# A 20-product scheme for the first expert layer, with three accumulators moved to DRAM and more accumulation on ScalarE

## The chip, the cores and the metric

The kernel runs on one core of one Trainium2 chip. The metric is device time in microseconds for one launch. A profiled execution gives a trace of every instruction; TensorE is called PE in it, its weight loads PEld, VectorE DVE, ScalarE ACT, GpSimd POOL, and SP is the engine that issues most DMAs.

## The reference

Linear attention with the feature map elu + 1 is followed by a mixture of eight experts. The weights of the experts for a token come from a Sinkhorn iteration over all tokens, so they are known only when the attention of all tokens is done.

```python
# attention: 8 batches, 8 heads, 576 tokens, 64 per head
q_p, k_p = phi(q), phi(k)                       # phi(x) = elu(x) + 1
kv = einsum('bhsd,bhse->bhde', k_p, v);  z = sum(k_p, axis=2)
x = einsum('bhsd,bhde->bhse', q_p, kv) / (einsum('bhsd,bhd->bhs', q_p, z)[..., None] + 1e-06)
# x becomes 4608 tokens x 512
P = exp(x @ w_gate - max)                       # 4608 x 8
for _ in range(8):
    P /= P.sum(1, keepdims=True) + 1e-09
    P /= P.sum(0, keepdims=True) + 1e-09
    P *= N / E
for e in range(8):
    h = maximum(x @ w1[e], 0)                   # 512 -> 1024
    out += P[:, e:e + 1] * (h @ w2[e])          # 1024 -> 512
```

## The kernel before

**Order of work.** Everything is emitted by a planner, the class `_Plan`. A task has an engine (or a choice of two), a cost in us, dependencies, buffers that it takes from pools, and a priority; `run` goes through the tasks in planned time and emits the instructions of each engine in that order. [...] A table `ranks` overrides the priority or the engine of single tasks by their number. For TensorE the order of the expert part is written out by hand: the list `order` names the products of one unit and its neighbours, and a chain of dependencies makes the planner keep it.

**Stages.** The front computes the attention for one batch and four heads at a time and writes x, transposed and in fp16, to `xT`. Expert 0 runs while the front is still going on, with plain matmuls (`layer1`, L546, and `unit_plain`, L736), because its result can be scaled by P afterwards (L757). The Sinkhorn iteration runs on VectorE meanwhile. Then come experts 1 to 7, each in nine units of 512 tokens.

**A unit of experts 1 to 7.** Both layers use a scheme of 7 products in place of 8 for a 2x2 by 2x2 block product (the Strassen-Winograd form).

- First layer (`block7`): sums of x are made once, on VectorE (`x_blocks`, L579), and stored in DRAM in `xd`. For each unit SP loads 896 KB of them back (L598). Sums of w1 (`combos`, W, L783) are made once per expert. In two halves of the hidden columns, seven products of four 256-column matmuls each run in PSUM (L640). ScalarE copies partial results (L652, L656, L660) and does two of the four relus (L663, L666); VectorE does the other two as "add, then relu" from PSUM and SBUF (L669).
- Second layer (`unit`): VectorE makes four sums S of the hidden values (L816), 128x1024 each; T holds the sums of w2 (L795). Seven products of eight matmuls (L843) run in three banks, X, R and Z. Product 1 is copied once to seed Z (L878). Six results are then scaled by P and added to `acc`: five by VectorE in one operation from PSUM (L857), one by ScalarE, which scales into a buffer `st` (L864), and POOL, which adds it (L867).

The accumulators `acc` of all nine units lie in SBUF. The very last unit of expert 7 uses plain matmuls for its second layer (L736 and L720), so that its rows can be written out one after the other.

**Buffers.** PSUM has eight banks: two of the pool "hq", two of "att", ye0 and ye1 (X and R), ye2 (Z) and ye3 (the first layer's third bank). Weights are double-buffered and loaded by POOL (L207), cast from fp32 to fp16 on the way.

The only lines of the hand-written order:

```python
order = "y1 y5 y2 a7 y6 y3 a4 b1 b5 y7 b6 b3 b2 b7 A1 A5 y4 b4 A6 A3 A2".split()
final = "y1 y5 y2 y6 a7 y3 a4 b1 b5 y7 b6 b3 b2 b7 y4 b4".split()
```

Here y are second-layer products of the unit before, a and b the first-layer products of the two halves, and capitals belong to the next unit.

Of the kernel before, what the change touches and what calls it, by code (L numbers as in the profile page):

```python
# [16 lines left out]

class _Plan:
# [10 lines left out]

    def grp(self, pool):  # L30
        return {"pool": pool, "users": [], "tile": None}

# [19 lines left out]
    def run(self):  # L52
# [11 lines left out]
        def slot(t):  # L64
            r = t["ready"]
            seen = {}
            for g in t["acq"]:
                o, n = g["pool"]["order"], g["pool"]["n"]
                i = len(o) + seen.get(id(o), 0)
                seen[id(o)] = i + 1 - len(o)  # L70
                if i >= n:
                    for u in o[i - n]["users"]:
                        d = self.t[u]["done"]
                        if d is None:
                            return None
                        r = max(r, d + self.LAT.get(self.t[u]["on"], 0.06))
            return r

        while left:
# [28 lines left out]
            for g in t["acq"]:  # L108
                g["pool"]["order"].append(g)
# [13 lines left out]
def kernel(  # L123
# [10 lines left out]
    nc = tc.nc  # L134
# [21 lines left out]
    hpool = ctx.enter_context(tc.tile_pool(name="hpool", bufs=2))  # L156
# [5 lines left out]
    xpool = ExitStack()  # L162
    xp = xpool.enter_context(tc.tile_pool(name="xp", bufs=1, side="right"))

    xT = xp.tile([P, NDT, N], FP16, tag="xT", name="xT")
    NXB = 7 * 512
    xd = [dpool.tile([P, NXB], FP16, tag=f"xd{g}", name=f"xd{g}") for g in range(NG)]
# [6 lines left out]
    ones_t = const.tile([P, P], FP32, tag="ones", name="ones_t")  # L174

# [9 lines left out]
    p_att, p_hq, p_h = S_.pool(2), S_.pool(2), S_.pool(2)  # L185
    p_T, p_S, p_W, p_xs, p_xst, p_s2, p_s5 = (S_.pool(2) for _ in range(7))
    p_st = S_.pool(3)
    p_z = S_.pool(1)
    p_w1, p_w2 = S_.pool(2), S_.pool(2)
    p_ye = [S_.pool(1) for _ in range(4)]  # L190

    def load_w(ten, nm, pl, ap, cut, e, prio, parts=1, after=0.0, deps=()):
# [6 lines left out]
        for i in range(parts):  # L199
# [8 lines left out]
            ti = add(("pool", 1.0), fn, use=[g], prio=prio, deps=[tal])  # L208
            ts_.append(add(("dma", 6.0 / parts), lambda _: None, deps=[ti], use=[g], prio=prio, lat=2.6))
            w_last[0] = ti  # L210
        return g, [ts_[0], ts_[-1]]

    def load_w1(e, **kw):
        return load_w(moe_w1, "w1", p_w1, [[F, P], [F * P, NDT], [1, F]], 2, e, **kw)
# [22 lines left out]
    def att(b, g):  # L237
# [146 lines left out]
        for c2 in range(2):  # L384
# [8 lines left out]
            def f_xc(e, c2=c2, gx=gx):  # L393
                copy(e, xT[:, 2 * g + c2, S * b:S * b + S], gx["tile"])
# [6 lines left out]
    def logits(b2):  # L401
        gl = S_.grp(p_att)

        def f_l(_):
            gl["tile"] = aps.tile([P, NJ, E], FP32, tag="att", name="lg_ps")
            for i in range(NJ):
                for c in range(NDT):
                    nc.tensor.matmul(gl["tile"][:, i, :], lhsT=xT[:, c, ts(NJ * b2 + i, P)], rhs=wg_sb[:, c, :],
                                     start=(c == 0), stop=(c == NDT - 1))
# [8 lines left out]
    def sinkhorn():  # L418
# [9 lines left out]
        for it in range(8):  # L428
# [13 lines left out]
            gc = S_.grp(p_att)  # L442

            def f_c(_, gc=gc):
                gc["tile"] = aps.tile([P, E], FP32, tag="att", name="cs_ps")
# [61 lines left out]
    Zt = [None, None]  # L507

    def f_close(_):
# [4 lines left out]
        accp.append(ctx.enter_context(tc.tile_pool(name="combo", bufs=2)))  # L514
        for i, n in enumerate(("ye2", "ye3")):
            Zt[i] = yps.tile([P, 2, 256], FP32, tag=n, name=f"Z{n}")
            nc.tensor.matmul(Zt[i].rearrange("p a b -> p (a b)"), lhsT=warm[:, 0:P], rhs=warm, start=True, stop=True)
# [3 lines left out]
    hcount = [0]  # L521
    fin_prev = {}
    w_next = {}

    def layer1(e, g):
        gw1, tw1, gw2, tw2 = w_t[e]
        bs = range(512 * g // S, (512 * g + 511) // S + 1)
        xd_ = [xt_done[(b, c)] for b in bs for c in range(NDT)]
        th = []
        gh = S_.grp(p_h)  # L530

        def f_ha(_):
            gh["tile"] = hpool.tile([P, NFT, 512], FP16, tag="h", name="h")
        tha = add(("none", 0.0), f_ha, deps=[prev_hq[0]], acq=[gh], prio=g - 400.0)
# [4 lines left out]
        for f, c0, c1 in jobs:  # L539
            ghq = ghqs[f]  # L540

            def f_hq(_, f=f, ghq=ghq, c0=c0, c1=c1):
                if c0 == 0:
                    ghq["tile"] = hqp.tile([P, 512], FP32, tag="hq", name="hq")
                for c in range(c0, c1):
                    nc.tensor.matmul(ghq["tile"], lhsT=gw1["tile"][:, c, ts(f, P)], rhs=xT[:, c, ds(512 * g, 512)],  # L546
                                     start=(c == 0), stop=(c == NDT - 1))

            def f_rl(_, f=f, ghq=ghq):
                nc.scalar.activation(out=gh["tile"][:, f, :], in_=ghq["tile"], func=AF.Relu)  # L550
# [4 lines left out]
            x_users.append(t1)  # L555
# [3 lines left out]
        return gh, [th, th]  # L559

    def x_blocks(g):
        bs = range(512 * g // S, (512 * g + 511) // S + 1)
        deps = [xt_done[(b, c)] for b in bs for c in range(NDT)]
        t0 = 512 * g
        gt_ = S_.grp(p_xst)

        def f_raw(_):
            nc.sync.dma_start(out=xd[g][:, 0:512].rearrange("p (c t) -> p c t", c=2), in_=xT[:, 0:2, t0:t0 + 256])
            nc.sync.dma_start(out=xd[g][:, 512:1536].rearrange("p (c t) -> p c t", c=2), in_=xT[:, 2:4, t0:t0 + 512])
        last = None  # L570
        for i in range(4):
            def f_T(_, i=i):
                if i == 0:
                    gt_["tile"] = accp[1].tile([P, 4, 2, 256], FP16, tag="xst", name="xst")
                T = gt_["tile"]
                b11, b12 = xT[:, 0:2, t0:t0 + 256], xT[:, 0:2, t0 + 256:t0 + 512]
                b21, b22 = xT[:, 2:4, t0:t0 + 256], xT[:, 2:4, t0 + 256:t0 + 512]
                a0, a1 = [(b12, b11), (b22, T[:, 0]), (b22, b12), (b21, T[:, 1])][i]
                nc.vector.tensor_tensor(out=T[:, i], in0=a0, in1=a1, op=ALU.subtract)  # L579
            last = add(("dve", 0.42), f_T, deps=deps + [t_close, last], acq=[gt_] if i == 0 else [], use=[gt_],  # L580
                       prio=g - 8.0)
            x_users.append(last)

        def f_st(_):
            nc.sync.dma_start(out=xd[g][:, 1536:NXB], in_=gt_["tile"].rearrange("p i c t -> p (i c t)"))
        ti = add(("sp", 0.45), f_st, deps=[last], use=[gt_], prio=0.0)
        out_ = [add(("dma", 1.5), lambda _: None, deps=[ti], use=[gt_], prio=0.0, lat=2.6)]
        ti = add(("sp", 0.9), f_raw, deps=deps + [t_close, ti], prio=0.0)
        out_.append(add(("dma", 1.0), lambda _: None, deps=[ti], prio=0.0, lat=2.6))
        x_users.append(out_[1])  # L590
        return out_

    def x_load(e, g):
        gr = S_.grp(p_xs)

        def fn(_):
            gr["tile"] = accp[1].tile([P, NXB], FP16, tag="xs", name="xs")
            nc.sync.dma_start(out=gr["tile"], in_=xd[g])  # L598
        ti = add(("sp", 0.1), fn, acq=[gr], deps=xd_done[g] + [t_close, xs_prev[0]], prio=e * NG + g)
        xs_prev[0] = ti  # L600
        return gr, add(("dma", 3.0), lambda _: None, deps=[ti], use=[gr], prio=e * NG + g, lat=2.6)

    def block7(e, g, gW, tW):
        gw1, tw1, gw2, tw2 = w_t[e]
        ui = e * NG + g
        gxs, txs = x_load(e, g)
        gh = S_.grp(p_h)
        th = [[], []]

        def f_ha(_):  # L610
            gh["tile"] = hpool.tile([P, NFT, 512], FP16, tag="h", name="h")
        tha = add(("none", 0.0), f_ha, deps=[prev_hq[0]], acq=[gh], prio=ui - 400.0)

        def A(i, j, gi):
            return lambda p, c: gw1["tile"][:, 2 * (j - 1) + c, ts(4 * (i - 1) + 2 * gi + p, P)]

        def W(i, gi):
            return lambda p, c: gW["tile"][:, i - 1, c, ts(2 * gi + p, P)]

        def Bx(o, w):  # L620
            return lambda c: gxs["tile"][:, o + w * c:o + w * c + 256]

        def T(i):
            return Bx(1536 + 512 * (i - 1), 256)
        B11, B21, B22 = Bx(0, 256), Bx(512, 512), Bx(768, 512)

        def pair(gi):
            gX, gR, gZ, gs2, gs5 = (S_.grp(p) for p in (p_hq, p_att, p_ye[3], p_s2, p_s5))
            kx = {id(gX): (hqp, "hq"), id(gR): (aps, "att")}
            f0 = 2 * gi  # L630

            def pm(lhs, rhs, g_, first, deps, pr):
                def f_m(_):
                    if first:
                        pl, tag = kx[id(g_)]
                        g_["tile"] = pl.tile([P, 2, 256], FP32, tag=tag, name=tag)
                    dst = Zt[1] if g_ is gZ else g_["tile"]
                    for p in range(2):
                        for c in range(2):
                            nc.tensor.matmul(dst[:, p, :], lhsT=lhs(p, c), rhs=rhs(c),  # L640
                                             start=(first and p == 0 and c == 0), stop=(c == 1), skip_group_check=True)
                return add(("pe", 0.436), f_m, deps=deps, acq=[g_] if first else [], use=[g_, gw1, gW, gxs],
# [363 lines left out]
```

The softmax here doesn't subtract the row's maximum and nothing guards it: scores larger than these inputs give would overflow.

## Time and profile before

| | |
|---|---|
| Device time, two runs | 970.89 and 974.2 us, median 972.55 |
| Span of the profiled execution | 970.4 us, 21442 instructions |
| Granted TensorE clock | 0.999 |
| Busy: PE, DVE, ACT, POOL | 959.5, 776.5, 575.0, 112.2 us |
| HBM read and written | 119.69 MB and 17.69 MB |

The span runs from the first to the last instruction of the profiled execution; the device time of a run contains a little more on both sides, and is here between 0.5 and 3.8 us longer than the profiled span. A busy time counts an engine once where two of its records overlap. The mean duration of an instruction in the groups is longer than its step in a full queue, because the next one starts before it ends.

### The profile page before, as it was taken

The numbers are of one execution on the slowest core, as the hardware profiler recorded it, in microseconds if no ns is written. First come the engines' busy times: TensorE is split into PE (matmuls) and PEld (weight loads), VectorE is DVE, ScalarE is ACT, GpSimd is POOL, SyncE is SP. The second block draws the span as 40 slices with busy tenths as digits, with TensorE's granted clock in tenths as the row PEclk, the third lists the DMA queues.
The fourth block names the chain that finished last, engine by engine and source line by source line (L and its number), as shares of the span: only waits on it lengthen the run. The fifth ranks groups of instructions, "written<-read, shape, count | busy, mean of one in ns | idle before, by whom it ended". The sixth has DMA issues, their size and how long they took to land.

```text
span 970.4 us, 21442 instructions
## 1 busy us (share of the span) xinstructions
PE 959.5 (99%) x8737; PEld 794.4 (82%) x8737; DVE 776.5 (80%) x1563; ACT 575.0 (59%) x1049; POOL 112.2 (12%) x158
## 2 busy tenths in 40 slices
PE   8999999999999999999999999999999999999998
PEld 4556564588888888888888888888888888888886
DVE  6899868988887888878887888878887888877775
ACT  6799945465555555555555555555555555555553
POOL 3000000101111111111111111111111111111110
PEclk9999999999999999999999999999999999999999
DMA  9986925472226222272226222272226322235554
GB/s 312 265 271 243 243 73 207 155 162 76 78 76 138 99 74 74 79 152 78 73 75 138 98 73 78 76 161 77 78 77 137 104 77 77 77 96 166 163 163 110
DMA packets 47188, 121.99 MB, mean 126 GB/s; under 512 B 4208, under 2 KB 18288, under 8 KB 47088
## 3 DMA queue, kind: packets, MB, share of 16 engines
q1 hardware_dynamic: 32208, 99.76, 30.2%
q0 software_dynamic: 14480, 20.33, 11.8%
q8 instruction: 68, 1.11, 0.4%
q10 hardware_dynamic: 400, 0.52, 0.2%
q14 instruction: 32, 0.26, 0.1%
HBM read 119.69 MB, written 17.69 MB: 142 GB/s over the span
## 4 chain that ended last, share of the span: by engine, by line
PE 92%; DMA 3%; ACT 3%; DVE 1%; issue 1%; POOL 0%; ACTq 0%; DVEq 0%; POOLq 0%
PE ye L843 33%; PE hq L640 23%; PE att L640 11%; PE ye L736 6%; PE Zye L640 6%; PE Zye L843 6%; PE hq L546 4%; DMA w<-in_moe_w_dram 2%; PE yw L481 1%; DMA kin<-in_k_dram 1%; PE xt_ps L390 1%; ACT eq L266 1%; ACT h L550 1%; PE kv_ps L309 1%; PE num_ps L374 1%
## 5 line engine op out<-in xcount | busy, mean ns | idle before, releaser
L857 DVE SCALAR_TENSOR_TENSOR acc<-ye,P_sb,acc 128x256 f32<-128x256 f32 x620 | 267.2, 479 | 128.2 <-PE ye L843 127.7
L640 PEld LDWEIGHTS <-W 128*128 128x128 f16 x2016 | 197.2, 98 | 23.6
L843 PEld LDWEIGHTS <-S 128*128 128x128 f16 x1984 | 194.1, 98 | 22.5
L843 PE MATMUL ye<-T,S 128*128 128x256 f16 x1488 | 192.9, 273 | 0.0
L640 PEld LDWEIGHTS <-w 128*128 128x128 f16 x1512 | 147.9, 98 | 18.5 <-issue 0.8
L666 ACT ACTIVATE h<-hq 128x512 f16<-128x512 f32 x126 | 75.2, 597 | 144.1 <-PE hq L640 144.1
L843 PEld LDWEIGHTS <-h 128*128 128x128 f16 x1488 | 145.6, 98 | 16.9
L867 POOL TENSOR_TENSOR acc<-acc,st 128x256 f32<-128x256 f32 x124 | 87.5, 727 | 621.4 <-ACT st L864 562.5
L640 PE MATMUL hq<-xs,W 128*128 128x256 f16 x1008 | 151.3, 273 | 0.0
L640 PE MATMUL att<-xs,W 128*128 128x256 f16 x1008 | 151.3, 273 | 0.0
L640 PE MATMUL hq<-xs,w 128*128 128x256 f16 x1008 | 141.0, 273 | 0.4 <-DVE h L669 0.3
L663 ACT ACTIVATE h<-Zye 128x512 f16<-128x512 f32 x126 | 75.2, 597 | 40.6 <-PE Zye L640 40.6
L864 ACT ACTIVATE st<-Zye,P_sb 128x256 f32<-128x256 f32 x124 | 52.0, 470 | 78.3 <-PE Zye L843 78.3
L669 DVE CUSTOM_DVE_ANT_0 h<-att,s 128x512 f16<-128x512 f32 x126 | 86.6, 687 | 11.4 <-ACT s L656 11.0
L656 ACT COPY s<-hq 128x512 f32<-128x512 f32 x126 | 73.4, 583 | 36.7 <-PE hq L640 36.7
L816 DVE TENSOR_TENSOR S<-h 128x1024 f16<-128x1024 f16 x124 | 85.2, 687 | 12.3 <-ACT h L666 12.3
L669 DVE CUSTOM_DVE_ANT_0 h<-hq,s 128x512 f16<-128x512 f32 x126 | 86.6, 687 | 0.2
L652 ACT COPY Zye<-hq 128x512 f32<-128x512 f32 x126 | 73.2, 581 | 17.5 <-PE hq L640 17.5
L736 PE MATMUL ye<-w,h 128*128 128x512 f16 x312 | 75.6, 379 | 1.9 <-DMA w<-in_moe_w_dram 1.4
L640 PE MATMUL Zye<-xs,w 128*128 128x256 f16 x504 | 75.7, 273 | 0.0
L660 ACT COPY s<-att 128x512 f32<-128x512 f32 x126 | 74.7, 593 | 0.0
L546 PE MATMUL hq<-xT,w 128*128 128x512 f16 x288 | 70.3, 379 | 0.9 <-ACT h L550 0.7
(95 smaller groups left out, 961.2 us busy)
## 6 DMA issues: line engine op xcount, KB each, us to landing
xs<-xd SPq DMA_DIRECT2D x63, 896.0 KB, 4.6
w<-in_moe_w_dram POOLq DMA_DIRECT2D x14, 1024.0 KB, 11.4
out_dram<-acc SPq DMA_DIRECT2D x67, 128.0 KB, 2.4
kin<-in_k_dram SPq DMA_DIRECT2D x14, 576.0 KB, 5.8
qin<-in_q_dram SPq DMA_DIRECT2D x14, 576.0 KB, 5.5
vin<-in_v_dram SPq DMA_DIRECT2D x14, 576.0 KB, 5.8
xd<-xst SPq DMA_DIRECT2D x9, 512.0 KB, 2.7
xd<-xT SPq DMA_DIRECT2D x9, 256.0 KB, 3.1
```

The source lines that it names most:

```text
L546: nc.tensor.matmul(ghq["tile"], lhsT=gw1["tile"][:, c, ts(f, P)], rhs=xT[:, c, ds(512 * g, 512)], start=(c == 0), stop=(c == NDT - 1))
L640: nc.tensor.matmul(dst[:, p, :], lhsT=lhs(p, c), rhs=rhs(c), start=(first and p == 0 and c == 0), stop=(c == 1), skip_group_check=True)
L656: nc.scalar.copy(out=gs2["tile"], in_=gX["tile"])
L660: nc.scalar.copy(out=gs5["tile"], in_=gR["tile"])
L663: nc.scalar.activation(out=hd(0, 0), in_=Zt[1], func=AF.Relu)
L666: nc.scalar.activation(out=hd(1, 0), in_=gX["tile"], func=AF.Relu)
L669: nc.vector._custom_dve(TENSOR_ADD_SAT, out=dst, in0=ps, in1=sb, s0=3.0e38, s1=0.0)
L736: nc.tensor.matmul(gy[tt]["tile"], lhsT=gh["tile"][:, f, ds(P * tt, P)], rhs=gw2["tile"][:, f, :], start=(f == 0), stop=(f == NFT - 1))
L816: nc.vector.tensor_tensor(out=Sx[:, i], in0=a0, in1=a1, op=op)
L843: nc.tensor.matmul(bank(g_)[:, s, :], lhsT=lhs(s, kk), rhs=rhs(kk), start=(new and s == 0 and kk == 0), stop=(kk == 3), skip_group_check=True)
L857: nc.vector.scalar_tensor_tensor(out=dst(), in0=bank(g_)[:, s, :], scalar=P_sb[:, gg, e:e + 1], in1=dst(), op0=ALU.mult, op1=ALU.add)
L867: nc.gpsimd.tensor_tensor(out=dst(), in0=dst(), in1=gst["tile"], op=ALU.add)
```

## The change

The first layer of experts 1 to 7 is computed in units of 768 tokens, six in all, with a scheme of 20 products in place of 24 for a block product of 4x2 (w1: four blocks of hidden columns, two of inputs) by 2x3 (x: two of inputs, three of tokens). The second layer keeps its units of 512 tokens and its seven products. Two first-layer units and three second-layer units make one round of 1536 tokens; `ORDER` lists the 61 products of a round, each with the round that it belongs to relative to the others, and this list replaces `order` and `final`.

- `A_SUM` lists 15 sums of w1 blocks, `B_SUM` 13 sums of x blocks; `A_OF` and `B_OF` say which operands a product takes. The x blocks are stored to DRAM one by one in the order of their use (`xd` is now three sets of ten tiles of four blocks) and loaded four at a time (512 KB), into three and later six buffers.
- `STEPS` lists what happens with the products of a first-layer unit: 2 seeds and 8 saves by ScalarE, 2 relus by ScalarE (`ev0`), 10 add-relus (`ev1`) and 2 additions to a saved value (`savex`) by VectorE. The products run in five PSUM banks, so ye3, hq and att are shared by eight short chains.
- Of the six scaled results of a second-layer unit, four go through ScalarE and `st` and two (products 5 and 6) through VectorE. For units 0 to 4 and 8, POOL adds what is in `st` to `acc` in SBUF, 512 columns at a time, and VectorE accumulates its two directly. For units 5, 6 and 7 the accumulator lies in DRAM (`accd`), VectorE also scales into `st`, and POOL issues an accumulating DMA. The SBUF space of these three blocks holds T and two S buffers.
- Expert 0's blocks are scaled by P on ScalarE instead of VectorE. The weights of experts 2 to 7 are loaded in quarters, one per unit. The last unit is no longer plain. The small Sinkhorn matmul uses ye2 in place of "att". `xT` is split in three tiles whose space is reused for `sb` (saved values), `st` and three xs buffers. Entries of `ranks` above task 659 are gone.

The core of the diff:

```diff
+PRODUCTS = [(3, [2, 7, 15]), (4, []), (6, [5, 8]), (4, [3, 4]), (5, [4, 9]), ...
+ORDER = [(53, -2), (7, -1), (19, -1), (36, -2), (18, -1), (50, -2), (51, -2), (9, -1), (54, -2), ...
+    DG = (5, 6, 7)
+    accd = {g: dpool.tile([P, 4, 512], FP32, tag=f"ad{g}", name=f"ad{g}") for g in DG}
...
-                nc.vector.tensor_scalar(out=acc[g][:, tt, :], in0=acc[g][:, tt, :],
-                                        scalar1=P_sb[:, gg, 0:1], scalar2=None, op0=ALU.mult)
+                nc.scalar.mul(out=acc[g][:, tt, :], in_=acc[g][:, tt, :], mul=P_sb[:, gg, 0:1])
...
+    def hk1(e, v, afs):
+        for p in uo:
+            def f_m(_, p=p, c=c, n=n, sx=sx, new=new):
+                for pf in range(2):
+                    for kt in range(2):
+                        nc.tensor.matmul(bank(c)[:, pf, :], lhsT=lhs(p, pf, kt), rhs=own["xs"][sx][:, n % XC, kt, :],
+                                         start=(new and pf == 0 and kt == 0), stop=(kt == 1), skip_group_check=True)
...
+        for i, (kind, c, dst, src, dp, de, sg) in enumerate(STEPS):
+            def f_e(_, i=i, kind=kind, c=c, dst=dst, src=src, sg=sg):
+                if kind == "seed" or kind == "save":
+                    ... nc.scalar.copy(out=o, in_=bank(c)) or nc.scalar.mul(out=o, in_=bank(c), mul=-1.0)
+                elif kind == "savex":
+                    nc.vector.scalar_tensor_tensor(out=own["sb"][...], in0=bank(c), ... in1=own["sb"][...])
+                elif kind == "ev0":
+                    nc.scalar.activation(out=o, in_=bank(c), func=AF_.Relu, scale=float(sg[0]))
+                else:
+                    nc.vector._custom_dve(TENSOR_ADD_SAT, out=o, in0=bank(c), in1=own["sb"][...], s0=3.0e38, s1=0.0)
...
+        def ev(g_, ti, dh, dep, on_act):
+            if gst is None:
+                ... two nc.vector.scalar_tensor_tensor into acc, as before
+            else:
+                def f_e2(_):
+                    for s in range(2):
+                        if on_act:
+                            nc.scalar.mul(out=dst, in_=bank(g_)[:, s, :], mul=sc)
+                        else:
+                            nc.vector.tensor_scalar(out=dst, in0=bank(g_)[:, s, :], scalar1=sc, scalar2=None, op0=ALU.mult)
+                def f_g(_):
+                    st = own["st"][:, gst["slot"]]
+                    if g in DG:
+                        nc.gpsimd.dma_start(out=half(accd[g], ti, dh), in_=st, accum_op=ALU.add)
+                    else:
+                        dst = half(acc[g], ti, dh)
+                        nc.gpsimd.tensor_tensor(out=dst, in0=dst, in1=st, op=ALU.add)
```

## The prediction

> **What bounds the kernel now.** I read the page first (busy shares, the chain of waits), then the stages of 20 us, then the groups, and last the timelines of single engines.
>
> ```profile
> PE 959.5 (99%) x8737; PEld 794.4 (82%) x8737; DVE 776.5 (80%) x1563; ACT 575.0 (59%) x1049; POOL 112.2 (12%) x158
> ...
> PE 92%; DMA 3%; ACT 3%; DVE 1%; issue 1%; POOL 0%; ACTq 0%; DVEq 0%; POOLq 0%
> ...
> 500.00:520.00 20.00, 20.00 (x185) 17.91 (x184) 15.57 (x31) 11.20 (x22) 2.67 (x5) 1.00 0.12 47
> ```
>
> TensorE is 92% of the chain, and in every slice from 120 to 940 us it is busy 20.00 of 20.00 (the last line: PE, PEld, DVE, ACT, POOL, clock, DMA share, GB/s). Busy PE need not be PE at its peak, so I count: the chain shows eight 256-column matmuls in 0.87 us, 0.109 each. A unit of 512 tokens has 56 + 56 of them, 12.2 us, and POOL's first additions of two units start 12.23 us apart. So there is no stall left; only fewer matmuls make the middle shorter, and each new stall costs its full length.
>
> ```profile
> 499.77 1.41 POOL L867 TENSOR_TENSOR acc<-acc,st 128x256 f32<-128x256 f32 x2 [10.81 <-ACT st L864]
> 512.00 1.42 POOL L867 TENSOR_TENSOR acc<-acc,st 128x256 f32<-128x256 f32 x2 [10.82 <-ACT st L864]
> ...
> 508.67 0.68 DVE L669 CUSTOM_DVE_ANT_0 h<-att,s 128x512 f16<-128x512 f32 x1
> 509.27 0.68 DVE L816 TENSOR_TENSOR S<-S,h 128x1024 f16<-128x1024 f16 x1
> 509.87 0.69 DVE L816 TENSOR_TENSOR S<-h 128x1024 f16<-128x1024 f16 x1
> 510.49 0.88 DVE L857 SCALAR_TENSOR_TENSOR acc<-ye,P_sb,acc 128x256 f32<-128x256 f32 x2
> 511.28 0.68 DVE L816 TENSOR_TENSOR S<-h,S 128x1024 f16<-128x1024 f16 x1
> ...
> 511.44 0.84 ACT L864 ACTIVATE st<-Zye,P_sb 128x256 f32<-128x256 f32 x2 [1.26 <-PE Zye L843]
> ```
>
> The second fence gives prices. Starts on a busy VectorE lie 0.60 us apart (a 0.68 us record overlaps the next one), 0.40 for half of an accumulation pair; xst sums start 0.35 apart at 179 us. ScalarE's copies start 0.50 apart at 502 us; a scaled pair takes 0.84. A POOL addition of 256 columns fills 0.71.
>
> [...]
>
> ```profile
> 181.79 10.38 DVE L757 TENSOR_SCALAR acc<-acc,P_sb 128x512 f32<-128x512 f32 x26
> ...
> 188.91 3.57 POOL L207 DMA_DIRECT2D w<-in_moe_w_dram  x1 [73.20 <-PE hq L546]
> ...
> L207 POOL DMA_DIRECT2D w<-in_moe_w_dram x18: 745/838/3570, 8.7 to 746.1; - x18
> ```
>
> An issue with a median of 0.84 us took 3.57 and ended at 192.48, just after VectorE's row of 26 ended at 192.17. The form that matters here, S on VectorE against an addition on POOL, never coincides in the kernel before: each addition starts as the fourth S ends (the S at 511.28 ends 511.96, POOL starts 512.00). [...]
>
> **The change, part by part,** in rounds of 1536 tokens (3 old units, 36.7 us; 21 rounds).
> 1. *Fewer matmuls.* First layer: 63 units x 56 = 3528 become 42 x 80 = 3360. The last unit loses its plain form: 24 of 512 columns and 16 of 256 (64 equivalents) become 56. Together 176 x 0.109 = **-19.2 us**. A round is now 40 x 0.4365 + 21 x 0.873 = 35.8 us.
> 2. *VectorE.* Before: 12 add-relus, 12 S, 30 accumulations, 8/3 W and T: 12 x 0.60 + 12 x 0.60 + 30 x 0.40 + 1.6 = 28.0 of 36.7 us. After: 24 add-relus and savex, 12 S, 12 accumulating or scaling reads, 5 weight sums at 0.35, 4/3 T: 14.4 + 7.2 + 4.8 + 1.75 + 0.8 = 28.9 of 35.8 (81%). It fits: nothing on the path by load alone.
> 3. *ScalarE.* 33 copies x 0.50 + 3 pairs x 0.84 = 19.0 becomes 27 x 0.50 + 12 x 0.84 = 23.6 of 35.8 (66%). Nothing by load. From the written order I took, for each product, the PE time between the one before it in its bank and itself: the shortest gaps are three slots of 0.4365 = 1.31 us, against 0.10 + 0.85 for a pair. They just hold.
> 4. *POOL.* Per expert 24 additions of 512 columns (1.41 each, as two of 256) and 18 accumulating issues and 8 weight issues at 0.84: 56 of 107 us. An addition is no longer placed behind the fourth S. A round has 18.3 two-input VectorE operations; additions hold POOL 31% of the time; a blocked one waits half of 1.41: 18.3 x 0.31 x 0.70 = 4.0 us of VectorE delay per round. Its idle 6.9 us can take this, and S has about 3 us between the last h and the first product that needs it; but VectorE's narrow waits (y6 to y7: 1.75 us with 1.1 needed) cannot take a whole block queued in front. Bounds: nothing to 2 us per round on PE. I take 0.25, **+5 us**.
> 5. *DMA.* The queue table (packets, MB, share of 16 engines' span; q1 is SP's, q0 POOL's):
>
> ```profile
> q1 hardware_dynamic: 32208, 99.76, 30.2%
> q0 software_dynamic: 14480, 20.33, 11.8%
> ...
> xs<-xd SPq DMA_DIRECT2D x63, 896.0 KB, 4.6
> ```
>
>    That is 0.302 x 970.4 / 99.76 = 2.94 us per MB for SP and 5.63 for POOL. A round loads 5.24 MB of xs: 15.4 us, in six buffers that are each due only every 21 us, against 4.6 us for a landing today: hidden. In units 5 to 7 come 18 accumulations of 0.26 MB and three weight quarters (4.4 us): 35.8 - 15.4 - 4.4 leaves 0.89 us for each. At SP's rate one takes 0.77 and all hide; at POOL's 1.48 they don't. I take the hidden end, since POOL's queue so far carried weights that are cast from twice the bytes they land as: 0.
> 6. *Start of the rounds.* 78 x sums replace 36 and 120 stores replace 27. Scaling expert 0's blocks leaves VectorE (36 x 0.40) for ScalarE. In the first full round TensorE has only 40 + 10 products, 26.2 us, and VectorE 14.4 + 4.8 + 1.6 + 1.75 + some 20 late sums x 0.35, about 30. Bounds 0 to 6; **+3 us**. The front loses the tuned ranks of tasks above 659; PE waits little there now, bounds -1 to 4; **+1 us**.
> 7. *Last round.* y7, P16, y4, y5, y1, y3, y6, y7, y2, y4, y5, y3 stand close: a pair on ScalarE or VectorE needs about 1.1 us from product to product, and what stands between covers 0.44, 0.87, 0, 0.87 and 0: 0.6 + 0.2 + 1.1 + 0.2 + 1.1 = **+3.2 us**. The last block then goes ScalarE pair, POOL addition (0.95 + 1.41) where one VectorE operation of 0.48 stood: **+1.8 us**.
>
> Sum against the profiled span: 970.4 - 19.2 + 5 + 3 + 1 + 3.2 + 1.8 = 965.2. The median of the runs shown, 972.55, lies 2.15 above that span, so 967.4, say **967 us**.
>
> **Rivals.**
> - *All hidden:* additions fall beside harmless work, the start costs nothing: 967 - 5 - 3 - 1 = 958, and 955 if the last round overlaps better. For it: PE has no stall in the whole middle today, so an order laid by these same durations can hold. Against: three engines get fuller at once.
> - [...] half of the 4.0 us per round reaches TensorE: 2.0 x 21 = 42 for my 5: 1004. It decides once a blocked S or sum pushes an add-relu or y6's reads past their gap in most rounds. For it: the blocked 3.57 us issue. Against: the 3 us of room before S is needed.
> - *Accumulations in DRAM are slow:* at 1.48 us each, units 5 to 7 want 46.4 us of DMA in 35.8. Six st buffers take up about a third of the 10.6; the rest makes ScalarE and VectorE wait for a buffer, and TensorE for them: 7 x 7 = 49: 1016. It decides above 0.89 us each.
>
> **How the numbers follow.** Forecast 0.48 (958 to 985), all hidden 0.13, lock 0.19, DMA 0.20. About 2% is what a measurement of this kernel tells from no change: faster means under 953.1, slower over 992. The matmuls alone give 2.0%, so faster takes the all-hidden case at its best: 0.05. Slower is most of the lock and of the DMA case: 0.32. Same 0.63. The range goes from 953 to 1015: 0.03 stays below it, half of the DMA case and a little of the lock, 0.15, above.
>
> **What would show it.** Right: 8584 PE instructions, PE busy 20.00 per 20 us in the middle with 35.8 us from round to round, S at 0.68, VectorE near 80%, POOL near 50%. Lock: S, AF or POOL additions far above 0.68, 0.41 and 1.41, or gaps of up to a microsecond in front of S, then PE waiting for VectorE. DMA: ScalarE or VectorE waiting for a DMA of `ad`, in units 5 to 7 of each expert only, with rounds of unequal length. If rounds last 35.8 and the total is still above 985, my account of the ends is wrong; if all rounds are longer alike, items 2 and 3 are.

## The result, and the profile after

The changed kernel takes 1104.93 us (median of 2 runs, 1100.89 to 1108.98) against 972.55 before: the ratio is 1.136, with a 95% interval of 1.125 to 1.147. The forecast was 967, its range ended at 1015: both are wrong. Where the two runs of a kernel lie more than 1.5% apart, which happens twice below, the faster one is compared and no interval is given.

The page of the changed kernel: busy times, DMA queues, the chain of waits, the DMA issues.

```profile
PE 976.9 (88%) x8584; PEld 790.3 (71%) x8584; DVE 873.1 (79%) x1545; ACT 670.8 (61%) x1332; POOL 406.6 (37%) x364
...
q1 hardware_dynamic: 71632, 162.69, 44.6%
q0 software_dynamic: 49328, 53.37, 31.2%
...
PE 39%; DVE 26%; DMA 21%; issue 8%; POOL 2%; ACT 2%; POOLq 0%; DVEq 0%; SPq 0%; ACTq 0%
DMA ad<-st 17%; PE b L852 14%; PE ye L955 11%; DVE S L928 7%; DVE h L891 7%; PE ye L674 4%; PE hq L633 4%; DVE acc L976 3%; PE Zt L955 2%; DVE sb L881 2%; DMA w<-in_moe_w_dram 2%; DVE xst L724 2%; POOL ad L994 2%; DVE T L807 1%; DMA xs<-xd 1%
...
ad<-st POOLq DMA_DIRECT2D x126, 256.0 KB, 7.3
```

TensorE has the 8584 instructions that the forecast counted, 153 fewer than before. Its share of the chain falls from 92% to 39%: the accumulating DMAs into the DRAM accumulators (`ad<-st`) hold 17% and VectorE 26%. The profiled span is 1107.2 us. Of the 136.8 that it is longer, TensorE is busy for 17.4 longer (fewer matmuls, yet more busy time) and idle for 119.4 longer (1107.2 - 976.9 = 130.3 us idle, against 970.4 - 959.5 = 10.9). The device time of a run is 1.8 us longer than its own span (1108.98 against 1107.2); the 0.5 to 3.8 us given for the kernel before compare different executions.

Stages of 20 us of the changed kernel (PE, PEld, DVE, ACT and POOL busy, granted clock, DMA share, GB/s):

```profile
400.00:420.00 20.00, 20.00 (x185) 17.92 (x184) 17.00 (x27) 14.14 (x29) 9.12 (x9) 1.00 0.58 173
440.00:460.00 20.00, 15.99 (x146) 14.04 (x144) 14.02 (x28) 11.86 (x26) 8.66 (x9) 1.00 1.05 243
460.00:480.00 20.00, 14.71 (x117) 12.09 (x116) 14.95 (x23) 9.18 (x20) 8.22 (x7) 0.91 0.84 183
520.00:540.00 20.00, 20.00 (x185) 17.91 (x184) 15.21 (x26) 13.06 (x28) 8.81 (x8) 1.00 0.65 182
```

The stages are unequal, and the pattern comes back once per expert: other stages with a DMA share above 1 lie at 300, 560, 680, 820 and 940 us. (The share adds up the times of packets and can pass 1, so it is read as a load here.) Where it is 1.05 TensorE loses 4.0 us of 20, and in the stage behind it 5.3, at a granted clock of 0.91. The waits say who stands (us in total, times, longest):

```profile
POOL ad L994 <- DMA ad<-st: 60.4, 22, 5.9
...
ACT st L985 <- DMA ad<-st: 32.6, 13, 6.0
...
DVE st L987 <- DMA ad<-st: 30.1, 7, 6.9
...
PE ye L955 <- ACT st L985: 28.2, 10, 5.7
PE ye L955 <- DVE st L987: 21.8, 8, 5.3
PE ye L955 <- DVE T L807: 15.8, 6, 2.7
PE ye L955 <- DVE acc L976: 12.5, 16, 1.2
PE b L852 <- ACT sb L877: 11.9, 12, 1.5
```

ScalarE and VectorE wait for a DMA of `ad`, and TensorE for what they scale into `st`: that is the sign that the forecast gave for its DMA rival. The sign of its lock rival, VectorE waiting beside GpSimd's additions, is there too, in the row of VectorE's S additions (min/median/max ns) and in the timelines of VectorE and GpSimd:

```profile
L928 DVE TENSOR_TENSOR S<-h x126: 673/684/2381, 220.1 to 1079.7; 128x1024 f16<-128x1024 f16 x126
...
347.49 1.65 DVE L928 TENSOR_TENSOR S<-S,h 128x1024 f16<-128x1024 f16 x1
352.13 1.76 DVE L928 TENSOR_TENSOR S<-h,S 128x1024 f16<-128x1024 f16 x1
...
347.16 3.10 POOL L997 TENSOR_TENSOR acc<-acc,st 128x512 f32<-128x512 f32 x2 [1.16 <-ACT st L985]
351.68 1.65 POOL L997 TENSOR_TENSOR acc<-acc,st 128x512 f32<-128x512 f32 x1 [1.41 <-DVE acc L976]
```

The S that begins at 347.49, just after GpSimd's addition began at 347.16, takes 1.65 us in place of 0.68.

### The profile page after: what moved, and what is told of

Read it like the earlier page. It is cut to its first block, busy times and chain, and to the rows that moved or that the text cites. A ratio compares the mean times of both kernels' runs of the same rounds, so it can differ in the third digit from the quotient of the medians.

```text
span 1107.2 us, 22439 instructions
## 1 busy us (share of the span) xinstructions
PE 976.9 (88%) x8584; PEld 790.3 (71%) x8584; DVE 873.1 (79%) x1545; ACT 670.8 (61%) x1332; POOL 406.6 (37%) x364
## 3 DMA queue, kind: packets, MB, share of 16 engines
q0 software_dynamic: 49328, 53.37, 31.2%
HBM read 175.13 MB, written 61.34 MB: 214 GB/s over the span
## 4 chain that ended last, share of the span: by engine, by line
PE 39%; DVE 26%; DMA 21%; issue 8%; POOL 2%; ACT 2%; POOLq 0%; DVEq 0%; SPq 0%; ACTq 0%
DMA ad<-st 17%; PE b L852 14%; PE ye L955 11%; DVE S L928 7%; DVE h L891 7%; PE ye L674 4%; PE hq L633 4%; DVE acc L976 3%; PE Zt L955 2%; DVE sb L881 2%; DMA w<-in_moe_w_dram 2%; DVE xst L724 2%; POOL ad L994 2%; DVE T L807 1%; DMA xs<-xd 1%
## 5 line engine op out<-in xcount | busy, mean ns | idle before, releaser
L852 PE MATMUL b<-xs,AF 128*128 128x256 f16 x2520 | 344.0, 276 | 18.5 <-ACT sb L877 11.9
L891 DVE CUSTOM_DVE_ANT_0 h<-b,sb 128x512 f16<-128x512 f32 x420 | 277.6, 682 | 96.7 <-PE b L852 63.9
L997 POOL TENSOR_TENSOR acc<-acc,st 128x512 f32<-128x512 f32 x168 | 229.4, 1379 | 318.4 <-ACT st L985 286.8
L852 PEld LDWEIGHTS <-AF 128*128 128x128 f16 x2520 | 249.8, 99 | 56.9 <-issue 23.6
L985 ACT ACTIVATE st<-ye,P_sb 128x256 f32<-128x256 f32 x378 | 158.4, 470 | 131.2 <-PE ye L955 89.0
L994 POOL DMA_DIRECT2D ad<-st x126 | 138.2, 1268 | 193.6 <-ACT st L985 74.8
L852 PE MATMUL b<-xs,w 128*128 128x256 f16 x840 | 131.5, 281 | 8.2 <-DMA xs<-xd 6.5
L877 ACT COPY sb<-b 128x512 f32<-128x512 f32 x168 | 98.7, 588 | 57.0 <-DVE h L891 47.5
L879 ACT ACTIVATE sb<-b 128x512 f32<-128x512 f32 x168 | 100.4, 597 | 50.2 <-PE b L852 31.3
L976 DVE SCALAR_TENSOR_TENSOR acc<-ye,P_sb,acc 128x256 f32<-128x256 f32 x168 | 74.6, 475 | 33.2 <-ACT sb L877 19.6
L955 PE MATMUL ye<-w,S 128*128 128x256 f16 x504 | 67.7, 279 | 31.2 <-DVE st L987 21.0
L987 DVE TENSOR_SCALAR st<-ye,P_sb 128x256 f32<-128x256 f32 x84 | 36.5, 475 | 42.6 <-DMA ad<-st 30.1
```

The costliest lines, as they stand in the source:

```text
L852: nc.tensor.matmul(bank(c)[:, pf, :], lhsT=lhs(p, pf, kt), rhs=own["xs"][sx][:, n % XC, kt, :], start=(new and pf == 0 and kt == 0), stop= ...
L877: nc.scalar.copy(out=o, in_=bank(c))
L879: nc.scalar.mul(out=o, in_=bank(c), mul=-1.0)
L891: nc.vector._custom_dve(TENSOR_ADD_SAT, out=o, in0=bank(c), in1=own["sb"][:, sb[src[0]]["slot"]], s0=3.0e38, s1=0.0)
L955: nc.tensor.matmul(bank(g_)[:, s, :], lhsT=lhs(s, kk), rhs=rhs(kk), start=(new and s == 0 and kk == 0), stop=(kk == 3), skip_group_check=True)
L976: nc.vector.scalar_tensor_tensor(out=dst, in0=bank(g_)[:, s, :], scalar=P_sb[:, gg, e:e + 1], in1=dst, op0=ALU.mult, op1=ALU.add)
```

## Experiments

Three theories went in. A: the accumulating DMAs hold the staging buffers, and ScalarE, VectorE and TensorE stand behind them. B: GpSimd's additions hold up VectorE's additions of S and T (S took up to 2381 ns, with a median of 684). C: the start of the rounds costs some 30 us of its own.

**Leave out one, the other, both.** Edits: `dma_start(... accum_op=ALU.add)` becomes `pass` (first run), `gpsimd.tensor_tensor(...)` becomes `pass` (second), both (third).

> Leaves out the accumulating DMAs of the three DRAM accumulators (units 5 to 7 of experts 1 to 7: 126 blocks are not added), everything else as in the changed kernel. Theory A (the accumulating DMAs, issued back to back in three neighbouring units, hold the staging buffers, and ScalarE, VectorE and then TensorE stand behind them; the clock drops after each such gap): about 1015 us, with the waits of ScalarE and VectorE for a DMA of ad gone, every 20 us stretch of units 5 to 7 at 18 to 20 us of busy TensorE and a mean granted clock back near 0.99. Theory B ([...] the 673 ns additions of S take up to 2381 ns, and TensorE waits for S and T): above 1085 us. Theory C (the start up to 360 us costs the 30 us, independent of both): the first 240 us unchanged in this run.

> Leaves out GpSimd's additions into the SBUF accumulators (the four staged blocks of every pass in units 0 to 4 and 8 are scaled but not added); the accumulating DMAs stay. Theory A: 1080 to 1095 us, the waits for ad unchanged. Theory B: about 1010 us, S back to 690 ns in the mean, and the waits for ad much smaller, as VectorE would catch up. If the two act in a chain (VectorE late from the lock, then the staging buffers late), about 1050.

> Leaves out both the accumulating DMAs and GpSimd's additions. What stays over the ideal of 8.95 rounds is the start (theory C), the lengthened end and the clock. Theories A and B together with C: 975 to 985 us. If the start costs nothing of its own: 955 to 960 us. If VectorE's and ScalarE's own load on the new scheme were the bound: above 1000 us.

Measured:

| | additions in | additions out |
|---|---|---|
| accumulating DMAs in | 1104.93 | 1054.21 (1.084 [1.078, 1.090] of before) |
| DMAs out | 1035.87 (1.065 [1.060, 1.070]) | 976.06 (1.002 [0.999, 1.006]) |

Read along rows and columns: the DMAs cost 69 to 78 us, the additions 51 to 60, and together 129, nearly their sum. A and B are both right, side by side. They do not act in a chain: with the additions left out, GpSimd, ScalarE and VectorE wait for `ad` about as much as in the changed kernel (59.0, 40.6 and 26.8 us against 60.4, 32.6 and 30.1). TensorE's waits divide in the same way. Without the DMAs those for `st` all but vanish (0.5 us), while those for T, `acc` and `sb` stay (15.7, 12.1, 11.9); with neither, the latter are 0, 2.0 and 1.8.

Nearly all that the changed kernel loses against the one before is in these two, and C is small. With neither, TensorE is busy 20.00 of 20.00 in every stage from 240 to 940 us, as before, and S has lost its long cases (this kernel's page, stages and S row):

```profile
PE 946.1 (97%) x8584; PEld 780.0 (80%) x8584; DVE 797.8 (82%) x1545; ACT 669.5 (69%) x1332; POOL 41.3 (4%) x70
...
440.00:460.00 20.00, 20.00 (x186) 17.93 (x184) 15.05 (x26) 13.29 (x29) 1.76 (x3) 1.00 0.80 214
460.00:480.00 20.00, 20.00 (x186) 17.92 (x184) 16.94 (x32) 13.01 (x28) 0.00 (x0) 1.00 0.39 129
...
L928 DVE TENSOR_TENSOR S<-h x126: 679/684/694, 219.8 to 958.2; 128x1024 f16<-128x1024 f16 x126
```

Against this run the changed kernel's span is 132.9 us longer: 30.8 of it is the same 8584 instructions running longer (976.9 - 946.1), 102.1 is more idle time. The mean granted clock is 0.969 against 0.994. The longer instructions lie where the clock was lowered: from 240 to 1080 us, 13 of 42 stages have a clock below 1.00, with 0.122 us of busy time per matmul, against 0.109 in the other 29 and 0.108 with neither. Read in steps of 2 us, the clock behind the gap of 3.99 us that ends at 464.94 is 0.74 from 464 to 466 us, 0.50 from 466 to 468 and 0.91 from 468 to 470; from 466 to 468 TensorE has 11 matmuls in place of 20 or 21.

The length of a gap alone does not tell whether the clock falls: in the changed kernel it fell to 0.50 behind one of 2.48 us (984.93 to 987.41), and stayed at 1.00 behind those of 3.21 us (up to 340.14) and 3.05 us (up to 445.69). The stages with the longer instructions are those with the lowered clock, so most of the 30.8 us reads as a second bill of the same gaps; no run here held the clock while keeping the gaps.

**What in the DMA costs: the accumulating.** `, accum_op=ALU.add` is dropped, so that the DMA overwrites.

> The DMA of a scaled block to the DRAM accumulator overwrites instead of accumulating (the sum of experts is left out for units 5 to 7); same queue, same bytes from the staging buffer, same waits. If the price lies in the accumulating (reading the old value and adding): q0's share falls from 31% to about 20% and the time to 1036 to 1050 us, as without these DMAs. If it lies in GpSimd's queue and the landing time of any such DMA: little change, 1085 to 1105.

Measured: 1035.69 us, the same as without these DMAs (1035.87). Queue q0, the issues and their landings, with plain stores (first fence) and without any (second; q0 then carries the weights and six loads of q, k and v):

```profile
q0 software_dynamic: 25136, 53.37, 20.6%
...
L994 POOL DMA_DIRECT2D ad<-st x126 | 87.2, 701 | 175.0 <-ACT st L985 101.3 <-DVE st L987 49.6 <-DMA ad<-st 13.4
...
ad<-st POOLq DMA_DIRECT2D x126, 256.0 KB, 4.6
```

```profile
q0 software_dynamic: 15056, 20.33, 11.7%
```

An estimate from these shares: the other transfers take 0.117 x 1035.9 = 121 us of all 16 engines, a plain store of 256 KB takes (0.206 x 1035.4 - 121) / 126 = 0.73 us of them, an accumulating one (0.312 x 1107.2 - 121) / 126 = 1.78 us. The same 53.37 MB go in 49328 packets instead of 25136, land in 7.3 us instead of 4.6, and an issue occupies GpSimd for 1268 ns instead of 701 in the mean. The same sum on the pages of the runs without additions and with spread DMAs (below) gives 1.7 to 2.0 us. What it is in an accumulating DMA that takes the time, the reading of the old value or the smaller packets, was not separated: the page counts 175.13 MB read from HBM in both kernels.

**Where they stand: three neighbouring units, or one in three.** Edit, with the buffers that take over the three accumulators' SBUF renamed alike:

```
-    DG = (5, 6, 7)
+    DG = (1, 4, 7)
```

> Full computation, the same DMAs and additions, but the three DRAM accumulators belong to units 1, 4 and 7 in place of 5, 6 and 7, so that a unit with accumulating DMAs is followed by two without. Theory A: the DMA load of such a unit, about 1.05 of its stretch, is averaged with its neighbours to 0.8, and the time falls to 1010 to 1040 us. Theory B: no change within 1%, since the additions of GpSimd are as many as before. If the staging buffers are too few to carry a queue of 6 blocks at 1.8 us each over one unit: 1060 to 1080.

> The three DRAM accumulators belong to units 1, 4 and 7, and GpSimd's additions into the SBUF accumulators are left out. It asks whether spreading alone hides the accumulating DMAs. If they only cost by coming in three neighbouring units: as with both left out, 976 to 985 us. If every accumulating DMA costs something where it stands (landing time, issue on GpSimd): 995 to 1010. If the additions and the DMAs together were what delayed the staging buffers: 976 to 985 as well, but then the stretches of the changed kernel with DMAs alone (the run without additions, 1054 us) would not have shown the loss.

Measured: 1045.94 us with the additions (the other run took 1061.79) and 992.44 without them (1.020 [1.016, 1.023] of before; 1054.21 with the DMAs in neighbouring units). Spreading the same DMAs gains 62 of the 78 us without the additions, and with them some 59 of the 69. The stages of the run without additions:

```profile
460.00:480.00 20.00, 20.00 (x185) 17.92 (x184) 16.36 (x28) 14.30 (x30) 6.04 (x6) 1.00 0.90 199
500.00:520.00 20.00, 20.00 (x186) 17.93 (x184) 16.79 (x30) 14.19 (x30) 8.83 (x9) 1.00 1.01 202
```

TensorE stays at 20.00 through stages with a DMA share of 1.01, so a full stage by itself stops nothing. This fits a kernel that stops when the demand stays above the engines' time until the six staging buffers are full; the number of buffers was not varied. The 16 us that stay lie before 320 us, where the first accumulations meet the start, and at the end.

**What in the additions costs: a memset in their place.** `nc.gpsimd.tensor_tensor(out=dst, in0=dst, in1=st, ...)` becomes `nc.gpsimd.memset(dst, 0.0)`.

> GpSimd's addition is replaced by a memset of the same 128x512 block (the four staged blocks of a pass in units 0 to 4 and 8 are not added): GpSimd still has an instruction per block, in the same order, but one that reads nothing from SBUF. [...] as with the additions left out, 1050 to 1060 us, S at 690 ns. Rival ([...] GpSimd's queue is what costs): above 1080, S above 800 ns.

Measured: 1053.88 us (1.083 [1.070, 1.096]), the same as with no instruction there (1054.21); S is back at 680 to 690 ns in the mean.

```profile
L928 DVE TENSOR_TENSOR S<-h 128x1024 f16<-128x1024 f16 x126 | 86.1, 683 | 1.2
L997 POOL MEMSET acc<- 128x512 f32 x168 | 85.9, 579 | 394.1 <-DVE acc L976 389.7 <-ACT acc L689 4.4
```

So beside GpSimd instructions that only write, S kept its length: 683 ns in the mean, 685 with no instruction there and 976 beside the additions. The memset is less than half as long as the addition (579 ns against 1379 in the mean), so the test is of the kind of instruction and, in part, of its length.

**Shorter additions.** One addition of 128x512 becomes two of 128x256:

```
-   nc.gpsimd.tensor_tensor(out=dst, in0=dst, in1=st, op=ALU.add)
+   for s in range(2):
+       nc.gpsimd.tensor_tensor(out=dst[:, s], in0=dst[:, s], in1=st[:, s], op=ALU.add)
```

> Full computation. Each GpSimd addition of 128x512 is made as two of 128x256, so that the same elements are added [...]. [...] a blocked S waits half as long in the mean, S (128x1024, without own reuse) goes from 976 ns to about 830, and the time falls by a third to a half of the 51 us that the additions cost: 1080 to 1090 us. Rival (the additions cost through GpSimd's own queue and the staging buffers they hold): GpSimd's work per block grows by the second instruction's overhead, so no gain or a loss: 1105 to 1115.

Measured: 1064.31 us (1.093 [1.085, 1.102]), 40.6 less than the changed kernel: more than expected, and with all the arithmetic. S falls from 976 to 757 ns in its commonest form. The next step, halves and quarters with the spread DMAs:

> Full computation: the DRAM accumulators belong to units 1, 4 and 7, and each GpSimd addition is made as two of 256 columns. If the two costs are separate as in the runs before (halving saves 40 us, spreading some 50 to 60 with the additions out): 1005 to 1020 us, above the kernel before. If the additions were late only because of the DMA burst: below 1000. If halves don't help once the DMAs are spread (GpSimd's issues of 1.1 us then stand between the additions): 1035 to 1055.

> As the run with halves and spread DMAs, but each addition is made as four of 128 columns. [...] a blocked VectorE addition waits at most some 0.4 us, and the time falls by a further 5 to 12 us. If the fixed part of each GpSimd instruction, or GpSimd's occupation, takes over: the same or slower by up to 15 us.

Measured: 1059.06 us (1.088 [1.083, 1.092]) with halves, and 1033.17 with quarters (the other run took 1052.85), against 1045.94 with whole additions. The two gains do not add: my expectation of 1005 to 1020 missed. Halves gain nothing here; whether quarters do rests on one run of each. GpSimd's and VectorE's timelines in the run with halves and spread DMAs:

```profile
458.54 1.08 POOL L994 DMA_DIRECT2D ad<-st  x1 [4.15 <-ACT sb L879]
459.14 3.28 POOL L998 TENSOR_TENSOR acc<-acc,st 128x256 f32<-128x256 f32 x4
...
459.43 3.54 DVE L928 TENSOR_TENSOR S<-h 128x1024 f16<-128x1024 f16 x1
...
L928 DVE TENSOR_TENSOR S<-h,S x63: 673/680/6605, 220.4 to 1038.7; 128x1024 f16<-128x1024 f16 x63
```

The S that begins at 459.43 waits not for one half addition but for four in a row, to 462.42. With DMAs in every third unit the issues of `ad` stand between the additions and wait (179.3 us for ScalarE in the run with whole additions, 74.8 in the changed kernel), and the additions behind them then come several at a time.

**Gaps in the row of additions.** A memset of a 128x8 scratch tile behind each addition:

> Full computation, DRAM accumulators in units 1, 4 and 7, additions in halves (1059 us without the gap). After every half addition GpSimd now has a memset of a 128x8 scratch tile, an instruction that reads nothing from SBUF. In the runs with spread DMAs a single S addition on VectorE took up to 6.6 us, as long as a whole train of GpSimd additions standing back to back. [...] the gap lets VectorE in after one half, S falls below 2 us at most, and the time to 1000 to 1030. If VectorE waits for the end of the queued train whatever stands between: no gain, 1055 to 1070, as GpSimd's trains get longer by the memsets.

> As the one before with additions of 128 columns (1043 us without the gap) and a memset after each. If gaps let VectorE in: 995 to 1020 us, S at most 1.5 us. If not: 1040 to 1065[...].

Measured: 1063.1 us (1.091 [1.075, 1.106]) and 1052.08 (1.080 [1.066, 1.094]): no gain. The S at the same place still waits for four additions, memsets and all (run with halves):

```profile
459.54 3.49 DVE L928 TENSOR_TENSOR S<-h 128x1024 f16<-128x1024 f16 x1
...
459.06 1.24 POOL L1000 TENSOR_TENSOR acc<-acc,st 128x256 f32<-128x256 f32 x1
459.81 1.22 POOL L1000 TENSOR_TENSOR acc<-acc,st 128x256 f32<-128x256 f32 x1
460.53 1.22 POOL L1000 TENSOR_TENSOR acc<-acc,st 128x256 f32<-128x256 f32 x1
461.26 1.21 POOL L1000 TENSOR_TENSOR acc<-acc,st 128x256 f32<-128x256 f32 x1
```

But a row of additions alone does not block. In the run with halves and neighbouring units, six stand in a row, and VectorE gets in between them, each time after less than one:

```profile
338.78 6.53 POOL L998 TENSOR_TENSOR acc<-acc,st 128x256 f32<-128x256 f32 x6
...
339.48 1.10 DVE L928 TENSOR_TENSOR S<-S,h 128x1024 f16<-128x1024 f16 x1
342.49 1.11 DVE L807 TENSOR_TENSOR T<-w 128x1024 f16<-128x1024 f16 x1
343.52 1.21 DVE L928 TENSOR_TENSOR S<-h,S 128x1024 f16<-128x1024 f16 x1
```

What the long waits have in common is a DMA issue of GpSimd directly ahead of the additions: its record has not ended (458.54 + 1.08 = 459.62 above) when the first addition's begins (459.14). From 235 to 1040 us, the S and T additions that waited more than 1.5 us beside GpSimd's additions (took more than 2.18 us) number 11 in the changed kernel, 1 with halves, 16 with spread DMAs and 18 with spread DMAs and halves. All of them met additions directly behind such an issue, of weights in the first two runs and of `ad` in the others. Where no issue stood directly ahead, none waited more than 1.1 us for whole additions or 0.54 for halves. Rows of additions directly behind an issue of `ad` number 1 and 2 with neighbouring units and 43 with spread ones. So spreading took load from the DMA engines and put the issues in front of the additions. Why an issue has this effect is open, and no run moved the issues away from the additions.

**The start.** On the run with both kinds left out, the scaling of expert 0's blocks goes back from ScalarE to VectorE (`nc.vector.tensor_scalar` for `nc.scalar.mul`).

> The run with both kinds of accumulation left out (976 us) is the base; here the scaling of expert 0's 36 blocks by their probability is done by VectorE (as in the kernel before) and no longer by ScalarE. In the base TensorE idles some 16 us between 180 and 230 us: about 6.3 us waiting for xs loads from DRAM, about 4 us for ScalarE's seeds and saves that stand behind these scalings. If ScalarE's queue matters: 971 to 973 us, the waits for ScalarE gone. If the loads and the late sums of x are the whole of it: 975 to 978. If VectorE's sums of x come later for it: above 978.

Measured: 975.80 us against 976.06: nothing. TensorE's waits there, from 180 to 235 us, are for the loads of x sums from DRAM:

```profile
PE b L853 <- DMA xs<-xd: 9.6, 3, 6.5
```

So ScalarE's scaling is not the limit. Which of the transfers of that stretch delays the loads was not separated.

No version beats the kernel before. The best with all the arithmetic is the one with quarters, at 1033 in one run and 1053 in the other. Even with both accumulations left out, the scheme is at 976, the same as before: TensorE is busy 13.4 us less (959.5 - 946.1), but idle 17.3 us more (974.3 - 946.1 = 28.2 against 10.9), 11.8 of it at the start.

## Why the prediction was wrong, point by point

- **Item 5, the DMAs: "I take the hidden end ... 0" failed.** It measured 69 to 78 us. The break-even of 0.89 us fits: at 0.73 (plain store) nothing is lost, at 1.78 much is. That rate lies outside both bounds (0.77 to 1.48). The guess that the software queue was dear because of its cast weights is in line with this: a plain store on it took 0.73, close to the 0.77 of SP's rate. The wrong step was to price an accumulation like a store; the accumulating itself, put at nothing, took 1.05 us more per DMA by the estimate from q0's shares. With 1.78 the rival's own sum gives 15.4 + 4.4 + 18 x 1.78 = 51.8 us for 35.8; less a third, 10.7 per expert, times 7 is 75: its mechanism holds, and its size with the measured rate.
- **Item 4, the lock: the blocked time was right, the part of it that reaches TensorE was not.** Forecast were 4.0 us of VectorE delay per round. That was my estimate, from a count of operations and the 1.41 us of an addition; that S waits for an addition was not shown by the kernel before, and what held the one issue of 3.57 us there was not tested. VectorE's busy time is 873.1 us, and 798.7 with the additions left out: 74.4 / 21 = 3.5 per round. I let 0.25 us per round through (+5) and bounded it at 2; the runs show 51 to 60 us, 2.4 to 2.8 per round, part of it by the lowered clock. The room of 3 us that S was said to have was the wrong place to look: TensorE's list of waits names no S. It waited for T, which the item did not name as at risk, and for VectorE's reads of its banks (`acc`), which it did. An addition of 512 columns took 1.27 us in the median for the 1.41 assumed.
- **The cases were treated as alternatives.** Lock (1004) and DMA (1016) reach TensorE through different waits (T, `acc` and `sb`; `st`), and the runs show them adding up: my own figures together give 967 - 5 + 42 + 49 = 1053, far outside the range. The 0.39 that I gave to one or the other should have held a case with both.
- **Item 6, start and front: +4 forecast.** From 100 to 270 us TensorE is busy 158.0 us with both kinds left out and 169.8 before: 11.8. Of this, 6.3 us are waits for the loads of x sums, which the item did not name.
- **Items 1, 2, 3 held.** 8584 instructions; with the accumulations out, VectorE is 84% and ScalarE 68% busy from 240 to 940 us (81 and 66 forecast), and TensorE has no gap there.
- **Item 7** shows in the last round with both left out as gaps of 0.49, 1.05 and 0.97 us in front of single products: of the size forecast.
- **Not foreseen:** the lower clock behind the gaps, most of the 30.8 us of longer busy time.

With item 4 taken out the forecast was 962; the run with neither is at 976. Some 8 us of that is the start. The rest is nearly all busy time: 13.4 us less than before, where item 1 had 19.2. The granted clock of 0.994 accounts for most of this, by an estimate: 0.006 x 974.3 = 5.8 us withheld, against 1.0 at the 0.999 before.

## What to carry to other kernels

Price an accumulating DMA apart from a plain one (1.78 against 0.73 us of 16 engines here), and compare the demand of each stretch as long as its buffers last, not of the whole span, with the engines' time. Before work is moved to GpSimd, list the VectorE instructions that take both inputs from SBUF, and what waits for each. In the changed kernel the 51 S that began during an addition of GpSimd (its last 0.3 us apart) took 1.15 to 1.76 us, for a median of 0.68 to 0.69; the 70 add-relus that did so, which read a PSUM bank, took 0.68 to 0.69. On this VectorE, 79% busy, 3.5 us per round were blocked and 2.4 to 2.8 reached the end. Shorter additions helped by 40.6 us where hardly any issue of an accumulating DMA stood directly ahead of them, and halves did not help where many did. When two rivals act through different waits, give their sum a chance too: here 69 to 78 us and 51 to 60 made 129.

## What the hardware showed that was not expected

- An accumulating DMA of 256 KB to DRAM took 1.78 us of 16 engines, 2.4 times a plain store's 0.73 (both estimates from the shares of q0: 31.2%, 20.6% and, with neither, 11.7%), and the queue's 53.37 MB went in 49328 packets instead of 25136.
- VectorE additions of 0.68 us took up to 6.6 us beside GpSimd's additions, and from 235 to 1040 us of four runs they waited more than 1.5 us only where these stood directly behind a DMA issue of GpSimd (46 cases). With a memset of 128x8 between the additions S still took 3.49 us there. Elsewhere none waited more than 1.1 us for whole additions or 0.54 for halves, and in a row of six halves VectorE got in after less than one.
- A gap in the matmuls was followed by a granted clock of 0.50, behind 2.48 us and behind 3.99 in the changed kernel, where the stage of 20 us from 460 us has a mean of 0.91; behind 3.05 and 3.21 us it stayed at 1.00.
